# Copying transposed q and k out of PSUM ahead of a region's exps, and three matmuls between AV groups

## The chip, the cores and the metric

The kernel runs on one core of one Trainium2 chip. The metric is the time of one execution on the device in microseconds (us), of which several are taken; the profile shows one more execution, instruction by instruction. Of the engines, PE is TensorE (matmuls; PEld its weight loads), DVE is VectorE, ACT is ScalarE, POOL is GpSimd, SP is SyncE.

## The reference

Block-causal attention (8 batches x 8 heads, 576 tokens, head size 64, blocks of 64), and on its output a maxout MoE layer.

```python
def _attn_ref(q, k, v):
    scores = (1.0 / np.sqrt(D)) * np.matmul(q, k.transpose(0, 1, 3, 2))
    # ... a query block sees its own and earlier key blocks ...
    attn = np.exp(scores - scores.max(-1, keepdims=True))
    attn = attn / (attn.sum(-1, keepdims=True) + 1e-09)
    return np.matmul(attn, v)

def _moe_ref(x, w1, w2, w_out):          # x: 4608 x 512, d_ff 1024
    return np.maximum(x @ w1, x @ w2) @ w_out
```

All inputs and the output are float32; the kernel computes in bf16 with float32 sums.

## The kernel before

PSUM is the memory that TensorE's results land in; here every tile has to be copied or otherwise read out of it before its buffer can be used again. AV stands for the product of the attention weights (the exps, tile `aT`) with v; DVE then divides it by the sums of the weights (a reciprocal, L435, and a multiplication, L436: "the division" below).

Heads are handled in pairs p = 0 to 31; two pairs make a group g. Each pass of the main loop (g = 2 to 15, "stage g" below) does the scores and exps of pairs 2g and 2g+1, the AV products of the two pairs before these, the transposes of q and k for group g+1, and in between a share of the MoE matmuls, handed out by `fill(n)`. `fill(n)` records n units of MoE work, where a unit is one matmul of 512 columns; narrower ones count less.

The program's order on each engine is the order of recording. All PSUM tiles but the scores come from one pool of four buffers, `ps_m`: the two halves of an MoE tile, an output tile, an AV group, each half of a transpose. Which buffer a tile gets is fixed when the program is built, from the order in which earlier tiles are read for the last time.

```python
ps_s = ctx.enter_context(tc.tile_pool(name="ps_s", bufs=2, space=bass.MemoryType.PSUM))
ps_m = ctx.enter_context(tc.tile_pool(name="ps_m", bufs=4, space=bass.MemoryType.PSUM))
# ...
def transposes(nm, g, copies):
    n = qk_n.pop((nm, g))
    pts = [ps_m.tile([P, RPP, NP], BF16, name=f"ps_{nm}T", tag="m") for _ in range(2)]
    for j in range(RPP):                         # the two halves take turns
        for i in range(2):
            # ... nc.tensor.transpose(pts[i][:, j, :], ...)
    def copy_out(which=(0, 1)):
        for i in which:
            t = (qT_r if nm == "q" else kT_r)[(2 * g + i) % NT]
            copies[i](out=..., in_=...)          # half 0 on DVE, half 1 on ACT
    return copy_out
# ...
def tile_2(p):                                   # tile_0, tile_1 alike
    u = ps_s.tile([P, 2, 512], FP32, name="ps_s", tag="s")
    # ... the score matmuls are recorded here, at once ...
    def out():
        exp(p, u, 512, 1024)                     # ACT; a second, small exp; masks on POOL
        # ...
    return out

def region(*tiles):
    for out in tiles:
        out()
# ...
def av_with(p, n):
    av(p, [0, 1])                                # first AV group: 6 matmuls, then division on DVE
    fill(n)
    av(p, [2, 3, 4])                             # second AV group: 24 matmuls, then division

for g in range(GPB, NG):
    a, b = 2 * g, 2 * g + 1
    # ... transposes of an earlier group's output; n = MoE work for this stage ...
    region(tile_0(a), tile_1(a))
    # ...
    lo, hi = n // 18, n * 2 // 9
    for p, tiles in ((a, lambda: (tile_2(a), tile_0(b))), (b, lambda: (tile_1(b), tile_2(b)))):
        fill(hi)
        if g > GPB:
            av_with(p - LAG, lo)
        else:
            fill(lo)
        copy_out = t_pair(p)                     # even p: q of group g+1, odd p: k
        region(*tiles())
        copy_out()
        # ... POOL work ...
    # ...
    fill(n - 2 * (lo + hi))
```

The softmax here doesn't subtract the row's maximum and nothing guards it: scores larger than these inputs give would overflow.

## Time and profile before

| | before |
|---|---|
| median time (3 runs) | 286.94 us |
| profiled span | 284.7 us |
| PE busy | 95% |
| one steady period (stages g=7 to 14, each) | 15.20 us |
| `lo`: units between the AV groups, g=2-6 / 7-14 / 15 | 1 / 2 / 3 |

How to read the lines: in a timeline row the first number is the start in us from the span's beginning, the second the time taken; then engine, source line, operation, output<-input, sizes and count. Square brackets tell how long the engine had been idle and what ended it. In the row that the windows view gives for a stretch of time, each engine has its busy microseconds and the number of instructions, in the order PE, PEld, DVE, ACT, POOL; then come the granted clock (1.00 is full), the DMA share and GB/s.

A stage starts where the first output transpose (L451) of that stage starts on PE; a stage's length is the distance to the next. Stage g=3 has no output transposes, so g=2 and 3 are given together. This "loop part", from the start of g=2 to the end, is what the change can reach. The recorded order of PE's instructions ahead of it is the same in both programs.

### The profile page before, as it was taken

To read this page: it belongs to the slowest core of one execution; us is meant where nothing else is said; L and a number is where in the kernel's file an instruction comes from. 1 tells how busy PE (TensorE), PEld (TensorE's weight loads), DVE (VectorE), ACT (ScalarE), POOL (GpSimd) and SP (SyncE) were. 2 spreads that over 40 slices of the span, in tenths; PEclk is the share of its full clock that TensorE was granted. 3 is DMA by queue.
4 is the path that set the end of the run, shared out by engine and by line. 5 is a ranking of instruction groups with operands and counts; after the bars stand their busy time and mean duration, and the time that the engine had idled before them with its cause. 6 is when DMAs were issued, how large, how long until landed. Compare 5 with 4: busy or idle time off the path is not lost.

```text
span 284.7 us, 7763 instructions
## 1 busy us (share of the span) xinstructions
PE 271.8 (95%) x3207; PEld 152.1 (53%) x3253; DVE 186.5 (65%) x386; ACT 140.8 (49%) x194; POOL 108.8 (38%) x271
## 2 busy tenths in 40 slices
PE   8799999899999999999999999999999999999995
PEld 3366666655555555555555464645555554444543
DVE  5867878758887576766666676667565765455430
ACT  3686567667566555573837556466454000110112
POOL 2996447764753634255253715462111000000000
PEclk9999999999999999999999999999999999999999
DMA  7999999959924893569264975176210111011114
GB/s 264 262 211 228 173 240 264 247 119 210 210 24 155 114 202 57 197 76 239 49 206 56 214 89 161 52 97 52 50 39 37 39 39 74 37 72 42 60 50 147
DMA packets 55939, 36.67 MB, mean 129 GB/s; under 512 B 38752, under 2 KB 43232, under 8 KB 55904
## 3 DMA queue, kind: packets, MB, share of 16 engines
q0 software_dynamic: 41728, 7.87, 34.9%
q1 hardware_dynamic: 13760, 27.66, 28.0%
q10 hardware_dynamic: 416, 0.66, 0.7%
q8 instruction: 25, 0.41, 0.6%
q14 instruction: 10, 0.08, 0.1%
HBM read 34.60 MB, written 9.44 MB: 155 GB/s over the span
## 4 chain that ended last, share of the span: by engine, by line
PE 81%; issue 2%; ACT 2%; DVE 1%; ACTq 0%
PE ps_h L197 39%; PE ps_y L215 21%; PE ps_o L429 9%; PE ps_s L321 6%; PE ps_qT L303 2%; PE ps_kT L303 2%; PE ps_xe L451 2%; ACT aT L345 1%; DVE g L206 1%; PE ps_y L231 1%; PE ps_s L339 1%; ACT qT L310 0%; ACT aT L401 0%; ACT kT L310 0%; PE ps_xo L453 0%
## 5 line engine op out<-in xcount | busy, mean ns | idle before, releaser
L197 PE MATMUL ps_h<-xT,w_sb 128*128 128x512 bf16 (+3 forms) x604 | 133.8, 357 | 4.0 <-issue 3.2
L345 ACT ACTIVATE aT<-ps_s 128x1024 bf16<-128x1024 f32 (+2 forms) x100 | 95.9, 993 | 62.1 <-PE ps_s L321 50.2
L197 PEld LDWEIGHTS <-w_sb 128*128 128x128 bf16 x640 | 57.3, 98 | 57.4 <-issue 8.4
L204 DVE CAST h<-ps_h 128x512 bf16<-128x512 f32 (+3 forms) x80 | 51.0, 637 | 29.3 <-PE ps_h L197 27.2
L215 PE MATMUL ps_y<-wo_sb,g 128*128 128x512 bf16 x273 | 65.5, 379 | 0.8 <-issue 0.5
L206 DVE TENSOR_TENSOR g<-h,ps_h 128x512 bf16<-128x512 bf16 (+3 forms) x80 | 50.7, 633 | 11.0 <-PE ps_h L197 8.9
L350 POOL MEMSET aT<- 64x128 bf16 x124 | 22.5, 200 | 91.6 <-ACT aT L345 90.8
L221 ACT COPY y<-ps_y 128x512 f32<-128x512 f32 x31 | 18.3, 591 | 71.4 <-PE ps_y L215 56.7
L429 PEld LDWEIGHTS <-aT 128*128 128x128 bf16 x960 | 37.0, 98 | 15.0 <-issue 3.9
L215 PEld LDWEIGHTS <-g 128*128 128x128 bf16 x280 | 27.0, 98 | 32.1 <-issue 1.1
L429 PE MATMUL ps_o<-vv,aT 128*128 128x65 bf16 x960 | 40.0, 194 | 0.5 <-DVE g L206 0.3
L133 POOL DMA_DIRECT2D vv<-in_v_dram x40 | 33.7, 847 | 0.5
L436 DVE TENSOR_TENSOR xp<-ps_o,rec 128x256 bf16<-128x256 f32 (+1 forms) x64 | 31.4, 491 | 2.2
L321 PE MATMUL ps_s<-qT,kT 64*128 64x64 bf16 (+6 forms) x344 | 31.8, 279 | 1.1 <-ACT kT L310 0.7
L435 DVE RECIPROCAL rec<-ps_o 128x4 f32<-128x4 f32 (+1 forms) x64 | 12.0, 187 | 23.6 <-PE ps_o L429 22.2
L187 POOL COPY g<-g 128x512 bf16<-128x512 bf16 x8 | 4.9, 614 | 38.5 <-DVE g L206 38.4
L129 POOL CAST kn<-kraw 128x1152 bf16<-128x1152 f32 x15 | 17.3, 1154 | 5.4 <-DMA kraw<-in_k_dram 5.3
L129 POOL CAST qn<-qraw 128x1152 bf16<-128x1152 f32 (+1 forms) x15 | 16.5, 1100 | 7.5 <-DMA qraw<-in_q_dram 7.4
L456 DVE COPY xT<-ps_xe 128x640 bf16<-128x640 bf16 (+2 forms) x18 | 8.1, 453 | 15.6 <-PE ps_xe L451 14.9
L321 PEld LDWEIGHTS <-kT 64*128 64x128 bf16 x344 | 13.6, 95 | 6.4 <-issue 2.8
L310 DVE COPY qT<-ps_qT 128x576 bf16<-128x576 bf16 x17 | 12.7, 749 | 1.2 <-PE ps_qT L303 1.2
L310 DVE COPY kT<-ps_kT 128x576 bf16<-128x576 bf16 x17 | 12.7, 749 | 0.5 <-PE ps_kT L303 0.5
(44 smaller groups left out, 142.4 us busy)
## 6 DMA issues: line engine op xcount, KB each, us to landing
qraw<-in_q_dram SPq DMA_DIRECT2D x16, 576.0 KB, 4.2
out_dram<-y SPq DMA_DIRECT2D x35, 256.0 KB, 2.7
kraw<-in_k_dram SPq DMA_DIRECT2D x15, 576.0 KB, 5.3
vv<-in_v_dram POOLq DMA_DIRECT2D x32, 128.0 KB, 5.2
w_sb<-in_moe_w_dram POOLq DMA_DIRECT2D x4, 256.0 KB, 7.0
w_sb<-in_moe_w_dram POOLq DMA_DIRECT2D x2, 512.0 KB, 11.3
wo_sb<-in_moe_w_out_dram POOLq DMA_DIRECT2D x2, 512.0 KB, 12.3
kraw<-in_k_dram ACTq DMA_DIRECT2D x1, 576.0 KB, 5.4
```

The source lines that it names most:

```text
L129: copy(out=n[:, j0:j1], in_=t[:, j0:j1])
L133: nc.gpsimd.dma_start(out=vv_r[b % NV][P - rows:, c, :, :D], in_=v[b, :, c * P:c * P + rows, :].rearrange("h p d -> p h d"),)
L197: nc.tensor.matmul(pt[:, :w], w_sb[:, c, f * P:(f + 1) * P], xT[:, c, t0:t0 + w], start=(c == 0), stop=(c == NDM - 1),)
L204: nc.vector.tensor_copy(out=h1[:, :w], in_=pt[:, :w])
L206: nc.vector.tensor_max(g[:, f, m:m + w], h1[:, :w], pt[:, :w])
L215: nc.tensor.matmul(py[:], g[:, f, s * P:(s + 1) * P], wo_sb[:, f, :], start=(f == 0), stop=(f == NFF - 1),)
L310: copies[i](out=t[:, :S].rearrange("q (p j) -> q p j", j=RPP), in_=pts[i].rearrange("q j p -> q p j"),)
L321: nc.tensor.matmul(ps[:, hh, col:col + w], kT[r, k0:k0 + P], qT[r, q0:q0 + w], start=True, stop=True,)
L345: nc.scalar.activation(out=aT_r[p % NA][:, :, a0:a0 + w], in_=ps[:, :, :w], func=AF.Exp, scale=scale,)
L350: (eng or nc.gpsimd).memset(aT_r[p % NA][BLK:, :, a0:a0 + BLK], 0.0)
L429: nc.tensor.matmul(po[:, gi, hh, :], a[:, hh, a0:a0 + P], vv[:, c, h0 + 2 * hh, :], start=(mm == 0), stop=(mm == n_mm - 1),)
L436: nc.vector.tensor_mul(xp[:, ts[0]:ts[0] + n, :, p % 2], po[:, :, :, :D], rec[:, :n].to_broadcast([P, n, 2, D]),)
```

## The change

Its intent: the second half of each transposed q or k leaves PSUM by a copy on ACT, recorded behind the region's exps. Recorded ahead of them, it should free its PSUM buffer earlier. And more MoE work between the two AV groups should give DVE and ACT time to free buffers. The whole diff, unchanged code cut at the dots:

```diff
-        lo, hi = n // 18, n * 2 // 9
+        lo, hi = max(3, n // 18), n * 2 // 9
         for p, tiles in (...):
             fill(hi)
 ...
             copy_out = t_pair(p)
-            region(*tiles())
+            outs = tiles()
             copy_out()
+            region(*outs)
```

The scores are still recorded ahead of the copy, in `tiles()`, so PE's order of scores and transposes doesn't change; ACT's order of copies and exps does.

## The prediction

> **What bounds the kernel now.** I read the engine shares and the chain first.
>
> ```profile
> PE 271.8 (95%) x3207; PEld 152.1 (53%) x3253; DVE 186.5 (65%) x386; ACT 140.8 (49%) x194; POOL 108.8 (38%) x271
> ...
> PE 81%; issue 2%; ACT 2%; DVE 1%; ACTq 0%
> ```
>
> TensorE is the bound: its own work is 81% of the chain that ends last. ACT and DVE together are 3% of the chain, some 8 us of 284.7; that is the most this change can touch, because it adds and removes no work on any engine.
>
> So the question is where PE stands still. "Busy" does not show it: a 512-column matmul is recorded as 379 ns, but follows the one before it after 216 ns, so a wait shorter than the overlap leaves no idle time. I went through the PE starts in the timeline and compared each distance with the same transition elsewhere. A distance of 432 between two 512-column matmuls is a missing record, not a wait: the weight loads count one more. Four kinds follow. First, steady state (one period of the main loop, two pairs of heads, is 15.20 us):
>
> ```profile
> 104.16 0.59 PE L321 MATMUL ps_s<-qT,kT 64*128 64x320 bf16 x6
> 104.65 1.02 ACT L345 ACTIVATE aT<-ps_s 128x1024 bf16<-128x1024 f32 x1 [2.58 <-PE ps_s L321]
> ...
> 106.00 1.02 ACT L345 ACTIVATE aT<-ps_s 128x1024 bf16<-128x1024 f32 x1
> ...
> 106.92 0.63 ACT L310 COPY qT<-ps_qT 128x576 bf16<-128x576 bf16 x1
> 107.01 0.13 PEld L197 LDWEIGHTS <-w_sb 128*128 128x128 bf16 x2
> 107.04 0.59 PE L197 MATMUL ps_h<-xT,w_sb 128*128 128x512 bf16 x2
> ...
> 107.60 0.90 PE L429 MATMUL ps_o<-vv,aT 128*128 128x65 bf16 x24
> ```
>
> The transposes of q were done at 104.1, but ACT takes their second half out of PSUM at 106.92, behind both exps. It ends at 107.55, and the second AV group, which has that PSUM buffer, starts at 107.60. The two matmuls ahead of it (2 x 216 from 107.04) would have let it start at 107.47. PE waits 0.135 us, once a period.
>
> Second and third, loop stages g=4 and g=5:
>
> ```profile
> 54.95 1.02 ACT L345 ACTIVATE aT<-ps_s 128x1024 bf16<-128x1024 f32 x1
> 55.87 0.63 ACT L310 COPY qT<-ps_qT 128x576 bf16<-128x576 bf16 x1
> ```
>
> ```profile
> 55.95 0.20 PE L303 MATMUL ps_kT<-ident,kn 64*128 64x64 bf16 x1
> 56.55 0.42 PE L303 MATMUL ps_kT<-ident,kn 64*128 64x64 bf16 x17 [0.40 <-ACT qT L310]
> ```
>
> ```profile
> 66.27 0.35 PE L429 MATMUL ps_o<-vv,aT 128*128 128x65 bf16 x6
> 66.46 0.38 PE L197 MATMUL ps_h<-xT,w_sb 128*128 128x512 bf16 x1
> 67.00 0.89 PE L429 MATMUL ps_o<-vv,aT 128*128 128x65 bf16 x24 [0.16 <-DVE g L206]
> ```
>
> At 55.95 the second transpose of k needs a buffer that the same late ACT copy holds: 0.60 us from start to start where 3 ns is normal. At 66.46 one lone MoE matmul stands between the AV groups, and the second group needs the buffer that DVE's max (66.26 to 66.95) frees: 0.54 less 0.216, 0.325 us. The same at 78.39 (g=6). Fourth, g=2, where the MoE matmuls are half as wide:
>
> ```profile
> 32.61 1.48 PE L197 MATMUL ps_h<-xT,w_sb 128*128 128x256 bf16 x12
> 34.41 0.44 PE L303 MATMUL ps_kT<-ident,kn 64*128 64x64 bf16 x18 [0.32 <-POOL kraw L118]
> ```
>
> Here PE comes to the transposes of k before POOL has cast k (33.20 to 34.35): the last distance is 0.588 where 0.205 is normal, 0.38 us.
>
> **What the Trainium skill says.** "Perfetto Trace Analysis", Identifying the Most-Contended Engine, says that matmul busy share is no measure of headroom, since matmuls are pipelined; the 379 against 216 ns agrees. Its Optimization Strategy says that the same gap repeating on the saturated engine can mean that a PSUM buffer is lacking; the 0.135 us that comes back every 15.20 us is such a gap. "TensorE: Matmul & The Clock Gate", Architectural detail, says that ACT and DVE are strict first-in first-out: that is why a copy recorded behind two exps can't pass them, and the order above (exp, exp, copy) agrees. "TensorEngine Tiling (Array Packing)", Key Properties, says that changing the tiling mode drains TensorE; the last 64-row matmul before a 128-row one takes about 0.1 us more than it streams (0.282 us for 448 columns). The change leaves these switches as they are, so I count none.
>
> **The change part by part.**
>
> *Copies ahead of the exps.* The order of ACT's queue changes for the 26 pairs that still transpose (p=4 to 29, g=2 to 14): copy, exp, exp instead of exp, exp, copy. DVE has no exps, so its half doesn't move. The copy costs 0.63 us before and after. It can start about 0.47 us after the transposes start (DVE's copy of the other half does: 34.41 to 34.88); then PSUM comes free at about 105.2 in place of 107.55, long before 107.47. The first exp loses 0.3 us for q (it could start at 104.65) and about 0.5 for k; their sum ends when it ended. The next scores, which need those exps' buffers, come more than a microsecond later in every stage but g=2.
>
> *At least three matmuls.* The count between the AV groups was 1 for g=2 to 6, 2 for g=7 to 14 and 3 for g=15 (ready work divided by 18, which I computed from the schedule). It becomes 3 throughout; those taken come off the run that closes the period, so the total is the same. A count is of 512-column matmuls: 3 means 5 or 6 of the narrow ones of g=2 and 3. From g=15 on, order and PSUM buffers are unchanged.
>
> I then followed each PSUM buffer of the changed program to the read that frees it, and set the durations of the rows above against each other:
>
> - g=2: the matmuls moved ahead (four of 256 columns at 0.109 us for q; then 15, seven of them of 320 columns at 0.136, in place of 12) fill 0.95 us before the transposes of k, so the 0.38 wait for POOL goes. Also 0.25 us at 37.94, a wait for the late copy of k. But the exps are late: copy 32.7 to 33.3, then 1.05 + 0.29 + 1.02 us to 35.7, while PE wants that buffer for scores at 35.47. A new wait of 0.28 replaces one of 0.09. Saved: 0.38 + 0.25 + 0.09 - 0.28 = 0.44.
> - g=3: waits of 0.18, 0.07, 0.14 and 0.32 us (the last for the late copy of q) go: 0.71.
> - g=4: 0.60 goes. With three matmuls there, an eight-matmul output tile ends between the AV groups, and DVE's copy of it (0.69 us, queued behind the first AV group's) holds the buffer for the transposes: about 0.1 us new, twice. Saved: 0.40.
> - g=5 and 6: 0.325 each goes; DVE's cast of the tile that now ends there holds the second buffer for k: about 0.1 new. Saved: 0.22 x 2 = 0.44.
> - g=7 to 14: 8 x 0.135 = 1.08. Here the buffers for the transposes of k are an output tile's, copied by ACT by 108.2 where they are wanted at 108.7, and an AV group's; I find no new wait.
>
> Sum: 0.44 + 0.71 + 0.40 + 0.44 + 1.08 = 3.07 us of the span, all on PE, hence all in the time. I take off 0.3 for waits that I haven't seen: 2.8. 286.94 - 2.8 = 284.1 us, 1.0% faster.
>
> **The rivals.** *A new wait takes the place of the old.* The exps move back 0.3 to 0.5 us, and there are only two score buffers. For it: g=2, where I already count 0.28. Against it: in a steady period ACT is busy 8.71 of 15.20 us, and the next scores come 1.1 us or more after the exps end. If it happened in each of 26 half periods at 0.2 us, the gain would turn into a loss of 2 us: 289.
> *DVE becomes the wait.* More tiles end between the AV groups, so casts stand ahead of the AV divisions. DVE is busy 10.2 of 15.20 us, 8.84 of 11.0 in g=3, so the early stages could lose what they gain: then only g=7 to 14 (1.08) and the late copies of g=2 to 4 (0.25 + 0.32 + 0.60) remain, less the 0.28 of g=2: 2.0 us, 284.9.
> *Nothing on PE, as the waits are hidden anyway.* If the distances I call waits were something else, the time would stay at 286.9. Against it: eight of them end within 50 ns after the same ACT copy.
>
> **Range and chances.** The median of before spread 0.6 us over three runs. The sum would be 3.8 if no new wait came and about 1.1 if the early stages gave nothing. So 284.1, from 283.0 to 285.8 eight times in ten. Faster by over 2% would need 5.7 us, more than all waits I found: 0.02. Slower by over 2% would need the first rival at its worst in both halves: 0.01. Within 2%: 0.97.
>
> **What would show it.** In the changed trace: ACT's copy of q or k directly after the transposes, ahead of two exps; a period of 15.07 us in place of 15.20; no PE distance of 0.35 at the second AV group; g=4 to 6 shorter by about 0.8 us in sum; from g=15 on the same length. It is wrong if scores wait for exps outside g=2, or if the transposes of k wait for a DVE cast by more than 0.1 us.

## The result, and the profile after

| | before | changed |
|---|---|---|
| median time, four runs each | 286.77 us | 282.49 us |
| profiled span | 284.7 us | 280.4 us |
| steady period | 15.20 us | 15.01 us |
| loop part, profiled | 254.90 us | 250.87 us |

The ratio is 0.985, 95% interval 0.9833 to 0.9867. A ratio here is the mean time of one kernel's runs over that of the other's runs of the same rounds, so not quite the ratio of the medians. Executions over 1.5% slower than the fastest of the same kernel are left out of the means. The result is correct. The gain is 4.3 us where 2.8 were predicted: right in direction and kind ("within 2%"), but 0.5 us below the predicted range.

The page of the changed kernel, engine shares and chain:

```profile
PE 269.3 (96%) x3208; PEld 151.5 (54%) x3253; DVE 185.7 (66%) x386; ACT 139.6 (50%) x194; POOL 107.7 (38%) x271
...
PE 91%; DMA 4%; issue 2%; ACT 1%; DVE 1%; POOL 0%; ACTq 0%
```

The work is what it was; ACT's part of the chain fell from 2% to 1%. PE is still the bound. Its 81% and 91% can't be compared: they are shares of the span, and the chain of the kernel before reaches back only to 37.3 us (86% of the span), that of the changed one to 0.7 us.

The timeline of a steady period of the changed kernel, the same place as the first timeline of the prediction:

```profile
101.06 0.44 PE L303 MATMUL ps_qT<-ident,qn 64*128 64x64 bf16 x18
...
101.61 0.64 ACT L310 COPY qT<-ps_qT 128x576 bf16<-128x576 bf16 x1 [2.48 <-PE ps_qT L303]
...
102.15 1.03 ACT L345 ACTIVATE aT<-ps_s 128x1024 bf16<-128x1024 f32 x1
...
103.50 1.02 ACT L345 ACTIVATE aT<-ps_s 128x1024 bf16<-128x1024 f32 x1
...
104.24 0.81 PE L197 MATMUL ps_h<-xT,w_sb 128*128 128x512 bf16 x3
...
104.89 0.90 PE L429 MATMUL ps_o<-vv,aT 128*128 128x65 bf16 x24
```

ACT copies 0.55 us after the transposes start, ahead of both exps, and is done at 102.25. The second AV group starts 0.65 us, three times 216 ns, after the first of its three matmuls: it waits for nothing.

Two steady periods in the windows view, first of the kernel before, then of the changed one:

```profile
99.36:114.56 15.20, 14.83 (x189) 8.26 (x192) 10.20 (x20) 8.71 (x13) 6.71 (x18) 1.00 0.66 133
```

```profile
96.41:111.42 15.01, 14.74 (x189) 8.27 (x192) 10.20 (x20) 8.62 (x13) 6.63 (x18) 1.00 0.70 135
```

Same number of PE matmuls, weight loads and DVE instructions, same clock (1.00), 0.19 us less time. The prediction had found 0.135 of these. Here, stage by stage, is where it and the traces part (lengths in us):

| stages | before | changed | saved | predicted |
|---|---|---|---|---|
| g=2 and 3 | 19.86 | 18.69 | 1.17 | 1.15 |
| g=4 | 10.63 | 10.05 | 0.57 | 0.40 |
| g=5 and 6 | 23.87 | 23.13 | 0.75 | 0.44 |
| g=7 to 14 | 121.60 | 120.06 | 1.54 | 1.08 |
| g=15 to the end | 78.94 | 78.95 | 0.0 | 0 |
| sum | | | 4.03 | 3.07, less 0.3 held back |

The rest, 0.26 us of the profiled runs' difference, lies ahead of the loop part, where the programs are the same.

Comparing each PE distance in one period of the two traces (as the prediction did) showed the missing 0.06: the transposes of q. In the kernel before:

```profile
102.97 0.89 PE L429 MATMUL ps_o<-vv,aT 128*128 128x65 bf16 x24
...
103.37 0.42 DVE L436 TENSOR_TENSOR xp<-ps_o,rec 128x256 bf16<-128x256 f32 x1
103.78 0.38 PEld L303 LDWEIGHTS <-qn 64*128 64x128 bf16 x18
103.78 0.50 PE L303 MATMUL ps_qT<-ident,qn 64*128 64x64 bf16 x18
```

The second half of this transpose takes the buffer of the first AV group, which DVE's division (103.37 to 103.79) frees. 18 transposes take 0.50 us where the changed kernel takes 0.44 (its row at 101.06): the second starts 68 ns after the first, where 3 or 4 ns is normal. **Theory:** the third matmul ahead of the second AV group moves the transposes 0.216 us later, past the division. **Rival:** all of the 0.19 comes from ACT's early copy, or each matmul added is worth something in itself.

### The profile page after: what moved, and what is told of

Read it like the earlier page. It is cut to its first block, busy times and chain, and to the rows that moved or that the text cites. A ratio compares the mean times of both kernels' runs of the same rounds, so it can differ in the third digit from the quotient of the medians.

```text
span 280.4 us, 7767 instructions
## 1 busy us (share of the span) xinstructions
PE 269.3 (96%) x3208; PEld 151.5 (54%) x3253; DVE 185.7 (66%) x386; ACT 139.6 (50%) x194; POOL 107.7 (38%) x271
## 4 chain that ended last, share of the span: by engine, by line
PE 91%; DMA 4%; issue 2%; ACT 1%; DVE 1%; POOL 0%; ACTq 0%
PE ps_h L197 43%; PE ps_y L215 22%; PE ps_o L429 11%; PE ps_s L321 8%; DMA vv<-in_v_dram 2%; PE ps_xe L451 2%; PE ps_qT L303 2%; DMA qraw<-in_q_dram 2%; PE ps_kT L303 2%; ACT aT L345 1%; PE ps_s L339 1%; PE ps_y L231 1%; PE ps_w L292 1%; DVE g L206 0%; POOL vv L133 0%
## 5 line engine op out<-in xcount | busy, mean ns | idle before, releaser
L197 PE MATMUL ps_h<-xT,w_sb 128*128 128x512 bf16 (+3 forms) x605 | 136.2, 357 | 1.7 <-issue 0.3
L429 PEld LDWEIGHTS <-aT 128*128 128x128 bf16 x960 | 37.3, 98 | 14.1 <-issue 1.3
L310 ACT COPY qT<-ps_qT 128x576 bf16<-128x576 bf16 x15 | 9.6, 638 | 29.4 <-PE ps_qT L303 29.4
L310 ACT COPY kT<-ps_kT 128x576 bf16<-128x576 bf16 x15 | 9.6, 638 | 15.0 <-PE ps_kT L303 15.0
```

The costliest lines, as they stand in the source:

```text
L197: nc.tensor.matmul(pt[:, :w], w_sb[:, c, f * P:(f + 1) * P], xT[:, c, t0:t0 + w], start=(c == 0), stop=(c == NDM - 1),)
L310: copies[i](out=t[:, :S].rearrange("q (p j) -> q p j", j=RPP), in_=pts[i].rearrange("q j p -> q p j"),)
L429: nc.tensor.matmul(po[:, gi, hh, :], a[:, hh, a0:a0 + P], vv[:, c, h0 + 2 * hh, :], start=(mm == 0), stop=(mm == n_mm - 1),)
```

## The experiments

All kernels below give a correct result. Those of one group ran on the same chip with shared runs of the kernel before, which there spread from 286.33 to 290.24 us (first two groups, median 287.3). Times of that spread don't resolve 0.2 us. Stage lengths from g=4 on repeat to 0.01 us among traces with the same order there (but for g=4 of e10, where weights were late), and the times are given beside them. Stages g=2 and 3 are less steady: with the changed kernel's order they took 18.69 us in two traces, but 18.37 to 18.76 in e4, e9, e10 and e12, whose loops started late. Of the kernel before there is one profile.

### e1: the changed kernel again

> The changed kernel once more, to settle how large the gain is and whether 0.26 us of it lies ahead of the main loop, where both programs are the same. Theory (the lead up to 29.8 us is chance of the start, such as when the first transfers land): the time is 4.0 us below before, give or take 0.3, and the start of the loop stages is as often late as early. Rival (the lead belongs to the change): 4.3 us, and the part ahead of the loop is again 0.26 us shorter than in before.

Measured: 282.47 us median of 6; ratio 0.9825 (0.9776 to 0.9875, widened by the spread of before). The medians of these rounds differ by 4.92 us, outside the expected 4.0 give or take 0.3, but before alone spread over 3.9 us there; the fastest runs differ by 4.02 (286.33 and 282.31). The loop part started at 29.81 us (before: 29.80) and took 250.86 us. So 4.03 us belong to the change, and the lead of 0.26 us was chance. In other runs below the start varied from 29.6 to 33.3 us, with PE waiting for the first v or the MoE weights to land (0.72 us for the weights in e7).

### e2: the copies ahead alone

```diff
-        lo, hi = max(3, n // 18), n * 2 // 9
+        lo, hi = n // 18, n * 2 // 9
```

> Copies ahead of the exps, but still 1 or 2 matmuls between the AV groups. Theory (buffers followed one by one; the 0.06 us by which the first transposes of q wait for DVE's division of the first AV group come from there being only two matmuls ahead of them): the 0.135 us wait at the second AV group goes, the 0.06 stays, so the period is 15.06 us; g=2 keeps its wait for POOL's cast of k (0.38); g=4 to 6 lose their 0.60 and 0.325 waits. Sum 2.9 us less than before, 283.9. Rival (all of the 0.19 per period is due to ACT's copy): period 15.01, over 3.3 us less.

Measured: 284.01 us median of 6; ratio 0.9878 (0.9825 to 0.9931). The loop part took 252.21 us, 2.69 less than before. Steady period, windows view and timeline of this run:

```profile
97.56:112.63 15.07, 15.07 (x193) 8.26 (x192) 10.20 (x20) 8.62 (x13) 6.65 (x18) 1.00 0.68 134
```

```profile
101.57 0.42 DVE L436 TENSOR_TENSOR xp<-ps_o,rec 128x256 bf16<-128x256 f32 x1
101.98 0.38 PEld L303 LDWEIGHTS <-qn 64*128 64x128 bf16 x18
101.98 0.50 PE L303 MATMUL ps_qT<-ident,qn 64*128 64x64 bf16 x18
...
102.59 0.64 ACT L310 COPY qT<-ps_qT 128x576 bf16<-128x576 bf16 x1 [2.31 <-PE ps_qT L303]
```

The 0.135 us wait is gone with the early copy alone, and the 0.50 of the transposes is still there, behind the same division. The rival (15.01) fails. The sum is 0.2 us short of the expected 2.9. In g=2 the wait for POOL, expected to stay at 0.38, was 0.03, as the cast of k started 0.37 us earlier in this run (32.83 us against 33.20); instead the scores waited 0.69 us for exps.

### e3 and e7: three matmuls alone

```diff
-            outs = tiles()
-            copy_out()
-            region(*outs)
+            region(*tiles())
+            copy_out()
```

> At least three matmuls, but the copies stay behind the exps. Theory: in steady state three matmuls push the second AV group to 0.13 us after the late copy's end, and the transposes of q come after the division, so both waits go without any early copy: period 15.01 us, as in the changed kernel. In g=2 the POOL wait goes (0.38). But in g=3 the second AV group now needs the buffer of the late copy of q and waits some 0.9 us, in g=5 and 6 some 0.55 each, g=4 some 0.1. Sum 2.1 us less than before, 284.7. Rival (the 0.135 us needs the early copy): period 15.14, sum under 1.2 us less.

Measured: 286.8 us median of 6, one of them slow; ratio 0.9957 (0.9909 to 1.0005). Its profile fell on a slow run (292.02 us), in which the weights for the MoE part landed 3 us late and the mean clock was 0.988; its steady periods are undisturbed at 15.01 us.

> At least three matmuls with the copies behind the exps, once more, as the first profile of it fell on a run whose first weights came 3 us late. Theory (from that trace: the late copies of q and k now hold back the second AV group by 0.92 us in g=3, 0.25 in g=4 and 0.57 each in g=5 and 6, and the transposes out by 0.5, 0.8, 0.2 and 0.2 us): with a normal start the loop part is 1.0 to 0.3 us shorter than before's 254.90, the period 15.01. Rival (the lost time was the late weights alone): 2 us shorter.

Measured: 286.62 us median of 4, ratio 0.9958 (0.9904 to 1.0013). The loop part took 254.47 us, 0.43 less than before, with the steady period at 15.01 us from g=8 on. The period is as e3's theory said, but its 2.1 us were far off. Even the 0.43 is in part luck: the loop of this run started late (30.87 us), and two waits for DVE at its start (0.15 and 0.09 us in the kernel before) are absent, so the edit's own gain is about 0.2 us (an estimate from these distances). Its stage g=5:

```profile
68.34 0.81 PE L197 MATMUL ps_h<-xT,w_sb 128*128 128x512 bf16 x3
...
68.88 0.63 ACT L310 COPY qT<-ps_qT 128x576 bf16<-128x576 bf16 x1
...
69.56 0.41 PE L429 MATMUL ps_o<-vv,aT 128*128 128x65 bf16 x8 [0.41 <-ACT qT L310]
```

Without the early copy, the third matmul changes which buffers the AV groups get: here the second AV group gets the buffer that the late copy of q holds, and waits 0.57 us. Beyond what e3's expectation had, the output transposes of g=4 to 7 now wait too, for the buffer of the late copy of k (the first of the four start at 50.70, 0.82 us after the start of the matmul ahead, where 0.31 is normal: 0.51 us). The 0.25 us in g=4, which the expectation gives to a late copy, ends by the trace 58 ns after a division on DVE. g=5 takes 13.09 us against 11.93 before and 11.57 in the changed kernel. So the two parts overlap in steady state, where either one removes the 0.135 us wait, and need each other in the early stages, where three matmuls alone lose what they gain.

### e4: two matmuls from g=7 on

```diff
-        lo, hi = max(3, n // 18), n * 2 // 9
+        lo, hi = max(3 if g < 7 else 2, n // 18), n * 2 // 9
```

> The changed kernel, but with 2 matmuls between the AV groups from g=7 on, as before; 3 in g=2 to 6. Theory: g=2 to 6 as in the changed kernel; in the 8 periods after that the 0.06 us wait of the transposes of q is back: period 15.06 us, 0.45 us more than the changed kernel. Rival (the third matmul does nothing in steady state): period 15.01, the time of the changed kernel within 0.15 us.

Measured: 283.27 us median of 6, 0.80 over e1 of the same rounds, more than the expected 0.45, but the traces resolve it better: period 15.07 us, and from the start of g=4 to the end 232.64 us against 232.17 of e1: 0.47 more. g=4 is equal (10.05). The rival fails; the third matmul's part in the 1.54 us of g=7 to 14 is 0.47.

### e9 and e10: which of the two places needs three

```diff
-                av_with(p - LAG, lo)
+                av_with(p - LAG, lo - (7 <= g < 15 and p == b))    # e9; e10: p == a
...
-        fill(n - 2 * (lo + hi))
+        fill(n - 2 * (lo + hi) + (7 <= g < 15))
```

> The changed kernel, but from g=7 to 14 three matmuls only ahead of the transposes of q, two ahead of those of k. Theory (the 0.06 us of each period is the wait of the transposes of q for DVE's division of the first AV group, and nothing else needs the third matmul): period 15.01 us, as with three in both. Rival (each half gains half of it): 15.04.

> The mirror of the run before: two matmuls ahead of the transposes of q, three ahead of those of k. Theory: period 15.07 us, as with two in both. Rival: 15.04.

Measured, the windows view of e9, then of e10:

```profile
97.48:112.49 15.01, 14.64 (x189) 8.34 (x192) 10.11 (x20) 8.62 (x13) 6.64 (x18) 1.00 0.70 138
```

```profile
113.00:128.06 15.06, 14.69 (x189) 8.35 (x192) 10.20 (x20) 8.57 (x13) 6.61 (x18) 1.00 0.62 130
```

Over g=7 to 14 e9 takes 120.05 us and e10 120.55: all of the difference is the matmul ahead of q's transposes, none the one ahead of k's.

What the transposes of q wait for, the traces tell: the profile names PE's second AV group as the releaser, not DVE. In the 36 stages that have this wait (10 each in before and e2, 8 each in e4 and e10) the second transpose starts 57 or 58 ns after the recorded end of the division, each time, while its distance from the recorded end of the last AV matmul runs from -9 to +2 ns; and in the changed kernel's steady periods it starts 64 or 65 ns before that end. So it is the division. No run delayed the division alone.

The times (two runs each, 284.79 and 284.01 us) are no use here: e9's second run took 286.35, and the start of e10's profiled run and its weights in g=4 were late.

### e11: the slack of the buffers in g=4

The prediction had counted new waits of 0.1 us, twice in g=4 and once each in g=5 and 6, for tiles that now end between the AV groups and are copied by DVE. In the changed trace the second transpose there starts 29 and 9 ns (g=4), 15 and 11 ns (g=5 and 6) after the first where 3 is normal, with DVE's copy or cast as releaser: the four waits came, but with 6 to 26 ns. The timeline of g=4 in the changed kernel:

```profile
50.74 0.42 DVE L436 TENSOR_TENSOR xp<-ps_o,rec 128x256 bf16<-128x256 f32 x1
...
51.09 0.68 DVE L221 COPY y<-ps_y 128x512 f32<-128x512 f32 x1
...
51.79 0.45 PE L303 MATMUL ps_qT<-ident,qn 64*128 64x64 bf16 x18
```

The copy starts 0.08 us before the recorded end of the instruction ahead of it (51.086 and 51.170 unrounded), and ends at 51.77, 0.03 us too late for the second transpose. To measure this slack:

```diff
+                if i < 2:
+                    nc.vector.memset(pad[:], 0.0)        # a tile that nothing reads
                 (dve if i < 2 else act)(out=y[:], in_=py[:])
```

> The changed kernel with a memset of 0.27 us on DVE ahead of each of its four copies of an output tile (g=4 and its neighbours), to measure the slack of the two buffers for which the prediction had counted a new wait of 0.1 us each. Theory (the copies end just in time in the changed kernel, 51.77 for transposes at 51.79, since consecutive instructions on DVE overlap by some 0.08 us, which the prediction's sums left out): g=4 grows from 10.05 to 10.4 us, 0.15 to 0.2 for each of the two. Rival (the buffers were free long before): no growth.

Measured: g=4 10.49 us against 10.05. In its timeline:

```profile
51.46 0.27 DVE L223 MEMSET pad<- 128x256 uint32 x1
51.65 0.63 DVE L224 COPY y<-ps_y 128x512 f32<-128x512 f32 x1
...
52.08 0.67 PE L306 MATMUL ps_qT<-ident,qn 64*128 64x64 bf16 x18
```

The copy ends at 52.28, and the second transpose of q, which would follow its first within 3 ns, starts 0.247 us after it, at 52.33; the transpose of k, 0.233 us. Less the 29 and 9 ns that were there before, the two grew by 0.44 us in sum, which is what the stage grew by. From the division's recorded end to the copy's it is 0.22 us more than without the memset, and each wait grew by 0.22. So the buffers are the ones that count and were free within a few hundredths of a microsecond of being wanted: the place of the predicted wait was right, its size an error of 0.07 to 0.09 us.

### e5: the wait in g=2

The changed kernel has one wait that the kernel before had only in part: in g=2 the scores wait for exps that now start behind a copy. The timeline there:

```profile
34.37 1.02 ACT L345 ACTIVATE aT<-ps_s 128x1024 bf16<-128x1024 f32 x1
...
35.45 0.23 PE L339 MATMUL ps_s<-qT,kz 64*128 64x64 bf16 x4
```

The exp ends at 35.39 and PE goes on at 35.45, 0.21 us later than the same step elsewhere. (The prediction had 0.28.)

```diff
             outs = tiles()
-            copy_out()
-            region(*outs)
+            if p == 4:
+                region(*outs)
+                copy_out()
+            else:
+                copy_out()
+                region(*outs)
```

> The changed kernel, but in the one pair p=4 (first half of g=2) q's copy stays behind the exps as before. Theory (the 0.21 us wait of the scores in g=2 of the changed kernel comes from the copy standing ahead of the exps there): the wait goes and the loop part is 0.2 us shorter than the changed kernel's, 250.7 from the first loop transposes to the end. Rival (the wait is the exps' own length and would be there anyway): no difference, 250.87.

Measured: 282.49 us median of 6, as e1. The wait for exps is gone, but g=2 and 3 take 18.80 us against 18.69: the transposes of k now get another buffer and wait 0.24 us for a cast on DVE, and the next stage's scores 0.15 us for an exp. The loop part is 250.97 us where 250.7 was expected. A miss: the wait moved, as the order of last reads deals out the buffers anew.

### e6: four matmuls

```diff
-        lo, hi = max(3, n // 18), n * 2 // 9
+        lo, hi = max(4, n // 18), n * 2 // 9
```

> The changed kernel with at least four matmuls between the AV groups. Theory (three already carry the transposes past the division, and no wait is left on PE in the steady period): the period stays at 15.01 us; the second AV group now wants a buffer that ACT's copy of an output tile frees at about the same moment, so at most 0.1 us is lost; the time is that of the changed kernel within 0.5 us. Rival (more matmuls keep helping): period under 14.95, over 0.5 us faster.

Measured: 283.40 us median of 4, 0.93 over e1; the loop part 251.86 us, 1.0 more. The period stays at 15.01 us, as expected. The loss is in the early stages, more than expected. Work that moves ahead of the second AV group is missing behind the scores, so the next scores come too early. PE's timeline at the start of g=5:

```profile
58.30 0.59 PE L215 MATMUL ps_y<-wo_sb,g 128*128 128x512 bf16 x2
...
59.99 0.39 PE L321 MATMUL ps_s<-qT,kT 64*128 64x64 bf16 x4 [0.49 <-ACT aT L401]
```

The scores at 59.12 go on only at 59.99, when ACT's exps have freed the second score buffer: 0.87 us where 0.16 is normal. The same costs 0.46 us at the start of g=3 and 0.19 at that of g=4. Of what was run (1 or 2, 3, and 4), three is the best; two in g=2 to 6 was not run.

### e8 and e12: a version beyond the changed one

In the last stage both kernels wait 0.26 us for DVE's max right after the first AV group behind the output transposes. Two units more in that stage let an MoE tile end earlier:

```diff
 def fill_of(g):
     if g == NG - 1:
-        return 54
+        return 56
```

> The changed kernel with q's copy of the pair p=4 behind its exps, and two matmuls more in the last stage, so that a tile of the MoE part ends two matmuls ahead of the last stages' transposes (the changed kernel waits 0.26 us there for a max on DVE). Theory: 0.2 + 0.26 us less than the changed kernel, loop part 250.4. Rival: the wait at the end only moves to another buffer: 250.7.

Measured (with e5's edit in it): 282.49 us median of 6; the loop part 250.75 us, where 250.4 was expected. From g=15 to the end 78.70 us against 78.93 of e1, and the 0.1 us of e5 lost in g=2 and 3.

> The changed kernel with two more matmuls in the last stage alone (the pair p=4 as in the changed kernel). Theory: the 0.23 us that the candidate gained after the last loop stage stay, without the 0.1 us that it lost in g=2: loop part 250.64 us, the fastest of all; in the time 0.23 us less than the changed kernel, which single runs don't resolve.

Measured (without e5's edit): 281.73 to 284.61 us, four runs, median 283.15; the loop part 250.32 us, less than the expected 250.64, but not all of it by the edit. The weights were late in its profiled run, so g=2 started at 30.40 and made up 0.3 us of that inside the stage; from g=4 to the end it took 231.94 us against 232.17 of e1. The 0.23 us hold, and this is the best version by its trace, but no times here resolve it from the changed kernel.

## Why the prediction was wrong

What held, each by its own step:

- *PE is the bound and only its waits count.* Work and clock are equal in the steady period, and in the changed trace the listed waits are gone, but for 0.21 us in g=2 and the few hundredths of point 2 below; that is where the 4.03 us come from.
- *The late copy on ACT holds PSUM, 0.135 us a period.* e2 removes that alone and the period falls by 0.13 (15.20 to 15.07).
- *g=2 and 3.* 1.17 us against 1.15; the exps do hold the scores in g=2, by 0.21 us where 0.28 were said. This is no luck of the sum: the listed waits of 0.38, 0.25, 0.18, 0.07, 0.14 and 0.32 us are all in the trace of before and none in that of the changed kernel.
- *From g=15 on the same length.* 78.94 and 78.95 us.
- *Rival one, scores wait for exps.* Only in g=2, and 0.06 us at the start of g=5; in the steady period ACT is busy only 8.62 of 15.01 us. By the letter, g=5 is one of the signs that the prediction named for being wrong (scores that wait for exps outside g=2), but it costs 0.06 of the 4.03 us. The failure lies elsewhere. e6 shows the rival real when PE brings the scores forward by one more matmul.

What failed:

1. *"g=7 to 14: 8 x 0.135 = 1.08."* The term should have been 8 x (0.135 + 0.06), measured as 8 x 0.19 = 1.54. The prediction went through PE's starts but missed one: in each of these eight stages the second transpose of q starts 61 to 68 ns after the first, where 3 or 4 is normal, and the profile names PE as its releaser. It is a wait for DVE's division of the first AV group (0.06 us, the term that the sum lacked). e2, e4 and e10 keep it (15.07), e9 and the changed kernel lose it (15.01). The same wait, 0.06 us, accounts for 0.12 us of g=5 and 6. So the third matmul did more than the prediction gave it.
2. *"About 0.1 us new, twice" in g=4, and "about 0.1 new" in g=5 and 6.* The four took 26, 6, 12 and 8 ns. The prediction doesn't print this sum, but DVE's recorded times laid end to end give the 0.1 in g=4; the trace has the copy start 0.08 us before the recorded end of the instruction ahead. e11 shows that 0.22 us more on DVE does bring 0.22 us of wait at each place in g=4, so the mechanism is right and the size was off by 0.07 to 0.09. For g=5 and 6 this is read from the trace alone (the cast in g=5 ends at 66.28, the transposes start at 66.32).
3. *"I take off 0.3 for waits that I haven't seen."* There were none on balance. What had not been seen was saved, not lost.

Two of the prediction's readings were loose, without consequence: PE's 81% is a share of the span, and so 94% of the chain, which covers 86%; and the copy of q, by the prediction's own 0.47 and 0.63 us from 103.78, would free PSUM at 104.9, not 105.2 (in the changed kernel 1.19 us after the transposes start). Of its signs, a period of 15.07 us and 0.8 us in g=4 to 6 were too small (15.01 and 1.32 us).

Together: 0.46 + 0.12 for the first, 0.36 for the second (0.17 in g=4 and, after the 0.12, 0.19 in g=5 and 6), 0.3 for the third; with the 0.02 of g=2 and 3 that is the 1.26 us between the 2.77 predicted (3.07 less 0.3) and the 4.03 of the loop part. The remaining 0.25 us of the 4.28 between the first medians matches the 0.26 us chance lead of that profile, and isn't in e1's; whether it was in the unprofiled runs too can't be told. Even without it, the time would have been 282.7 us, below the range, which had treated the sum as if the only surprises were losses.

## What to carry to other kernels

On a saturated TensorE with few PSUM buffers, list for each tile which read frees the buffer it gets; an order change helps by moving that read or by moving the moment at which the buffer is wanted, and either may deal the buffers out anew, so two edits don't add (here 2.69 and at most 0.43 us alone, 4.03 together). Sum waits down to a few hundredths of a microsecond if they recur every period, and look in the trace how far instructions overlap before laying recorded durations end to end (0.08 us decided here). Filling a gap with other work moves it from somewhere else: past three matmuls here, the scores of the early stages ran into their exps.

## What the Trainium skill lacked or had wrong

- "Perfetto Trace Analysis", Optimizing Scalar/DVE Operations, says that the write-acknowledgement half of a DVE or ACT instruction overlaps with the next one, and gives access overheads of ~51 to ~125 ns as about half of the profiled latency; it doesn't say how to shorten a sum of recorded times by it, nor when. Here a DVE copy out of PSUM starts 0.08 us before the recorded end of the instruction ahead, and an ACT copy 0.10 us before that of an exp (55.87 against 55.97), but the memset of e11, in the same place behind the division, starts 2 ns after that end.
- "TensorEngine Tiling (Array Packing)", Key Properties, says that a change of tiling mode drains TensorE and gives no size there. In these traces 64-row scores ahead of a 128-row matmul took 0.282 us where the last one streams 448 columns (0.189 us at the 216 ns of 512 columns): about 0.1 us. That the drain is what this time goes to is not shown here.
- "Perfetto Trace Analysis", Optimization Strategy, says that a repeating gap can mean missing buffers, and names buffer count and tile sizes; that buffers can be freed earlier or wanted later by order alone is not named there, though the paragraph ahead of it says to make what a gap waits for start sooner. Here both waits of the period went with four buffers unchanged (15.20 to 15.01 us).
- No page that I read says how a wait of PE shorter than its pipelined overlap looks in a profile: no idle time is recorded for the transposes of q, only 18 of them taking 0.50 us in place of 0.44.
